# Transposing the attention values there and back in two halves of two query blocks, in place of once for four

## The chip, the cores and the metric

The kernel runs on one core of a Trainium2 chip. The metric is the time of the whole program on the device, in microseconds; lower is better. The engines are named as in the profile: PE (TensorE; PEld is its weight loads), DVE (VectorE), ACT (ScalarE), POOL (GpSimd), SP (SyncE, which issues most DMAs).

## What is computed

Four layers in a row, A, B, A, B, on 2048 tokens of 576 features. A is causal attention in a sliding window of 256 tokens, with 32 heads of 18 features; B is a spectral filter. Both add to their input:

```python
def A(x):                       # x: 2048 x 576
    q, k, v = heads(layernorm(x) @ wqkv)          # 32 heads of 18
    s = q @ k.T * 18 ** -0.5, only where 0 <= query - key < 256
    return x + concat(softmax(s) @ v) @ wo

def B(x):
    X = rfft2(layernorm(x))
    return x + irfft2(X * (w_r + 1j * w_i))
```

The change is in A, so both attention layers meet it.

## The kernel before

**Groups and tiles.** A's 32 heads go in 8 groups of 4 (`n`), its tokens in 16 query tiles of 128 (`i`); x = 16n + i counts 128 such pieces of work. In a layer, projections (`pj`, L1109) make q and k of the groups, later ones while earlier groups are already attended to.

**One piece.** For each of its four heads (`pair`, `hp`) PE makes the scores S of a query tile (L1172, up to 384 keys wide) and DVE their maximum over the keys (L1174: `jk` is a by-product, `m` the result). Ten pieces later, with the maxima folded into q, PE makes the scores again with keys on the partitions (E, L1205), ACT takes exponentials into P (L1206), and POOL clears what the window excludes (L1208, L1211). Scores have three PSUM buffers, E three.

**Values.** `part(x, half)` (L1216) multiplies P with v: U, one PSUM bank of 128 partitions by 512 elements (`bufs=1`), takes four heads of 18 values and a sum in 32 partitions each, by four query tiles of 128. Each call issues matmuls of 128 or 256 queries for the four heads. After the fourth tile DVE transposes U into `us` (L1230, 128x512, in 32x32 blocks), so that the values of a token lie along the free dimension.

**From us to the output.** `later` (L1311) books three steps for bursts 1, 3 and 4 later: `divide` (L1238: DVE takes the reciprocal of the sums, and POOL multiplies, or DVE in the last group), `back` (L1244: DVE transposes us into o, 128x512, L1246), `store` (L1248: DMA of o). The last group's o goes straight into the room of the output projection. At the end of A `out.turn` (L782, three DVE instructions on L787 to L789 for the first blocks) prepares attended values, and `out.early` (L805) starts the output matmuls (`ops`, L802).

**Order.** The order is written by hand; engines run what is issued in that order. `bursts` (L1330) runs bursts of three (tile, pair, hp) steps: one score, three E, two more scores, then either value matmuls or projection steps, then the steps booked for this burst. While projections last, every burst of the set `values` (eight in 22) has the value matmuls of two query tiles and the others projection steps. When the projections are used up (`spread`, from 400.75 us on in layer 1), each burst takes some 8 to 24 value matmuls, and a burst ends ahead of a tile that begins the bank anew (x % 4 == 0). From x = 118 (MIX) on a plain loop without scores follows, `pv` for two tiles behind the exponentials, and then the output matmuls.

**Weights and tables.** `w_load` (L894) reads raw weights of a projection unit into one of two `wraw` buffers; `w_split` (L899) splits them into high and low parts, `wqh` and `wql`, and issues the load for the unit after the next. Late in a layer `const` (L754) puts five tables of the filter into the places of wraw, wqh and wql.

Of the kernel before, what the change touches and what calls it, by code (L numbers as in the profile page):

```python
# [8 lines left out]
F32 = mybir.dt.float32  # L9
F32R = mybir.dt.float32r  # L10
# [7 lines left out]
NF = 290  # L18
NT = 16
# [622 lines left out]
NQ = 8  # L642
# [54 lines left out]
def split_w(nc, raw, h, l, eng_l):  # L697
    nc.scalar.copy(h, raw)
    eng_l.tensor_sub(l, raw, h.bitcast(F32))
# [16 lines left out]
class Out:  # L716
# [36 lines left out]

    def const(self, k):  # L754

        t = ("wraw", "wraw", "wqh", "wqh", "wql")[k]
        d = self.bp.tile([128, 2, NF], F32R, tag=t, name=f"dc{k}", bufs=2)
        self.nc.sync.dma_start(d.bitcast(F32), self.dc_d[:, 2 * k:2 * k + 2].bitcast(F32))
        self.dcs.append(d)

# [105 lines left out]
def layer_a(tc, ident, eps, bp, big, src, dst, wqk_d, wv_d, wo_d, dc_d, gc_d, dram, copy, wvs, second, spectral, share):  # L866

    nc = tc.nc
    V, A, T, P = nc.vector, nc.scalar, nc.tensor, nc.gpsimd
# [14 lines left out]
    if True:  # L884
# [7 lines left out]
        wt, wraws = {}, {}  # L892

        def w_load(i):  # L894
            raw = bp.tile([128, 5, 128], F32, tag="wraw", name=f"wqr{i}", bufs=2)
            nc.sync.dma_start(raw.rearrange("p a b -> p (a b)"), wqk_d[i])
            wraws[i] = raw

        def w_split(i):  # L899
            raw = wraws[i]  # L900
            h = bp.tile([128, 5, 128], F32R, tag="wqh", name=f"wqh{i}", bufs=2)
            l = bp.tile([128, 5, 128], F32R, tag="wql", name=f"wql{i}", bufs=2)
            wt[i] = (h, l)
            split_w(nc, raw, h, l, V if i == 2 else P)
            if i + 2 < 9:
                w_load(i + 2)


        with tc.tile_pool(name="a1", bufs=2) as wp, ExitStack() as banks:
            pps = []  # L910
            if not second:
                wraw = wp.tile([128, 5, D], F32, name="wvraw", bufs=1)
# [163 lines left out]
        with ExitStack() as c2:  # L1076
            wp = c2.enter_context(tc.tile_pool(name="a2", bufs=2))
# [17 lines left out]
            def proj(i, c, bank=0):  # L1095
# [5 lines left out]
                def mm(s, k):  # L1101
                    wk, p, xk = k
                    if s == 7 and c == 2 and 0 < i < 8:
                        w_split(i + 1)
# [109 lines left out]
            us = {}  # L1214

            def part(x, half):  # L1216
                n, i = divmod(x, NT)

                e = i - i % 2
                j = (i - 1, i - 2 + 2 * (i % 2))[half]  # L1220
                q0 = e if j < i else i
                q1 = e + 2 if i - 1 == j else q0 + 1
                for h in range(4):
                    if j >= 0:
                        T.matmul(U[32 * h:32 * h + 19, (q0 % 4) * 128:(q0 % 4) * 128 + 128 * (q1 - q0)], vts[n][:, j, h],  # L1225
                                 pt[n, j][:, h, (q0 - j) * 128:(q1 - j) * 128],
                                 start=j == max(e - 1, 0), stop=j == i or (i == e and j == i - 2), skip_group_check=True)
                if half and i % 4 == 3:
                    us[n, i // 4] = u = wp.tile([128, NT, 32], F32, tag="us", name=f"us{n}_{i}", bufs=1)
                    V.transpose(u, U.rearrange("r (p n) -> r n p", n=NT))  # L1230

            def pv(x):
                part(x, 0)
                part(x, 1)

            os = {}

            def divide(n, c):  # L1238
                u = us[n, c]
                rc = wp.tile([128, NT, 1], F32, tag="rc", name=f"rc{n}_{c}", bufs=2)  # L1240
                V.reciprocal(rc, u[:, :, 18:19])
                (V if n == NQ - 1 else P).tensor_mul(u[:, :, 0:18], u[:, :, 0:18], rc.to_broadcast([128, NT, 18]))

            def back(n, c):  # L1244
                os[n, c] = o = wp.tile([128, NT, 32], F32, tag="o", name=f"o{n}_{c}", bufs=2)
                V.transpose(o, us[n, c])  # L1246

            def store(n, c, engines=None):  # L1248
                o = os[n, c].rearrange("r n p -> r (n p)")
                if n < NQ - 1:  # L1250
                    nc.sync.dma_start(op_d[n, :, c], o)
                    return
                for h in range(4):
                    (engines[h] if engines else nc.sync).dma_start(out.o7[18 * h:18 * h + 18, 512 * c:512 * c + 512], o[32 * h:32 * h + 18])
# [54 lines left out]
            steps = {}  # L1309

            def later(k, n, c):  # L1311
                for lag, f in zip(later.lags, (divide, back, store)):
                    steps.setdefault(k + lag, []).append((f, n, c))
                if c == 3:
                    for h in range(4):
                        steps.setdefault(k + (10 + 2 * h if n < NQ - 2 else 9 + h // 2), []).append((pack, n, h))

            later.lags = 1, 3, 4

            def lasting(p):  # L1320
                x, half = p
# [112 lines left out]
            U = pp.tile([128, 512], F32, tag="U", name="U", bufs=1)  # L1434
# [2 lines left out]
                f()  # L1437
                done += 1
            now = -(-4 * MIX // 3)
            later.lags = 1, 3, 4  # L1440
            ahead = [(max(now, 2 * k - now), f) for k in sorted(steps) for f in steps.pop(k)]
            for k, f in ahead:
                steps.setdefault(k, []).append(f)
# [20 lines left out]

            out.early(0, [bank(k, f"ops0_{k}") for k in ("pj", "S")], slice(0, 4))
            divide(NQ - 1, 3)
            back(NQ - 1, 3)
            store(NQ - 1, 3, (nc.sync, nc.scalar, P, nc.sync))
            out.early(0, None, slice(4, 11))
            out.early(1, [bank("S", f"ops1_{k}") for k in range(2)])  # L1470
# [55 lines left out]
```

## Time and profile before

| what | before |
|---|---|
| time, median of 3 runs | 1332.05 us (1330.12 to 1336.22) |
| time of the profiled execution | 1332.09 us |
| its span in the profile | 1330.0 us |
| first attention, from the first burst to the first output matmul | about 127 to 456.55 us |
| second attention | about 808 to 1137.16 us |
| us transposes (L1230) | 64, median 717 ns |
| o transposes (L1246) | 64, median 707 ns |
| granted TensorE clock, all but start and end | 9 tenths or more |

A row of a timeline gives the start, the duration, the engine, the line, the operation with output and inputs, and in brackets how long the engine stood idle before it and what ended that. Matmuls are pipelined, so the start of the next instruction tells when one is through better than its own duration does. A transpose's duration contains its way out of the engine, which overlaps with the next instruction; its occupancy is the distance to the next start. A row of a group gives busy time, mean duration, and idle time before the group's instructions with what ended most of it.

### The profile page before, as it was taken

What the parts mean: (1) busy time and instruction counts of PE and PEld (TensorE: products, weight loads), DVE (VectorE), ACT (ScalarE), POOL (GpSimd) and SP (SyncE); (2) the same over time, 40 slices, a digit from 0 to 9 for tenths busy, and PEclk for the clock granted to TensorE, in tenths of its full rate; (3) what the DMA queues carried; (4) which work ended last, traced back from release to release, by engine and by line L of the source; (5) the groups of instructions that cost most, each with busy time, mean ns of one, the idle gap of its engine ahead of it and who ended that gap; (6) DMA issues with size and microseconds to landing.
All of it is one profiled execution on the core that took longest, in us unless ns stands there. A gap on an engine that the chain in (4) does not pass through costs nothing.

```text
span 1330.0 us, 33103 instructions
## 1 busy us (share of the span) xinstructions
PE 1295.2 (97%) x10911; PEld 957.5 (72%) x10911; DVE 947.2 (71%) x3132; ACT 753.5 (57%) x1896; POOL 721.8 (54%) x1212
## 2 busy tenths in 40 slices
PE   9999999999999899999999999999999999999998
PEld 8986666566665599975999975666656654897587
DVE  5417888888889677766674148988888887675755
ACT  5622776677767645533355415677766678573233
POOL 2258666676667643566221295567667668213721
PEclk9999999999999999999999999999999999999999
DMA  6856766665657747688873468566656659497884
GB/s 205 215 161 204 220 206 190 214 201 186 188 162 241 222 120 227 191 282 254 265 251 76 102 208 225 184 213 178 192 175 192 189 173 296 140 346 254 283 260 155
DMA packets 179487, 274.22 MB, mean 206 GB/s; under 512 B 67743, under 2 KB 77727, under 8 KB 177989
## 3 DMA queue, kind: packets, MB, share of 16 engines
q1 hardware_dynamic: 166751, 242.45, 58.4%
q0 software_dynamic: 4912, 14.62, 4.3%
q10 hardware_dynamic: 7654, 15.03, 3.2%
q8 instruction: 88, 1.44, 0.5%
q14 instruction: 82, 0.67, 0.2%
HBM read 164.54 MB, written 114.81 MB: 210 GB/s over the span
## 4 chain that ended last, share of the span: by engine, by line
PE 82%; DMA 4%; POOL 4%; DVE 3%; issue 3%; ACT 2%; SPq 1%; DVEq 0%; ACTq 0%; POOLq 0%
PE pj L1109 18%; PE S L1172 13%; PE U L1225 11%; PE vps L1005 9%; PE ops L802 7%; PE E L1205 5%; PE po L274 4%; PE pq L524 3%; PE p L503 2%; PE pi L600 2%; PE pf L274 2%; PE pz L312 1%; POOL ks L1266 1%; POOL qs L1267 1%; DMA yd<-ye 1%
## 5 line engine op out<-in xcount | busy, mean ns | idle before, releaser
L1174 DVE CUSTOM_DVE_ANT_0 jk<-S,mask 128x384 bf16<-128x384 f32 (+2 forms) x1024 | 488.2, 525 | 72.3 <-PE S L1172 35.9
L1206 ACT ACTIVATE P<-E 128x384 f32<-128x384 f32 (+2 forms) x1024 | 408.2, 476 | 171.9 <-PE E L1205 134.4
L1172 PE MATMUL S<-ks,qs 63*128 63x384 f32 (+2 forms) x1024 | 280.1, 374 | 1.3 <-POOL qs L1267 0.3
L1208 POOL TENSOR_SCALAR_AFFINE_SELECT P<-P 128x512 f32<-128x512 f32 x256 | 163.2, 638 | 190.6 <-ACT P L1206 173.8
L1205 PE MATMUL E<-qs,ks 64*128 64x384 f32 (+2 forms) x1024 | 224.7, 372 | 6.4 <-ACT P L1206 3.7
L1172 PEld LDWEIGHTS S<-ks,qs 63*128 63x128 f32 x1024 | 145.6, 184 | 115.2 <-DVE m L1174 87.2
L1225 PE MATMUL U<-P,vq 128*19 128x128 f32 (+1 forms) x3840 | 188.6, 328 | 5.1 <-DVE us L1230 3.3
L1109 PE MATMUL pj<-xh,wqh 128*128 128x512 f32 x360 | 155.4, 432 | 0.4 <-DVE sg L1127 0.2
L1225 PEld LDWEIGHTS U<-P,vq 128*19 128x19 f32 x3840 | 95.6, 98 | 82.6 <-issue 16.0
L1211 POOL TENSOR_SCALAR_AFFINE_SELECT P<-P 128x512 f32<-128x512 f32 x224 | 142.8, 637 | 0.0
L1205 PEld LDWEIGHTS E<-qs,ks 64*128 64x128 f32 x1024 | 115.6, 185 | 22.5 <-ACT P L1206 16.5
L1109 PE MATMUL pj<-xh,wql 128*128 128x512 f32 x360 | 122.1, 416 | 0.0
L1109 PE MATMUL pj<-xl,wqh 128*128 128x512 f32 x288 | 119.6, 415 | 0.0
L802 PE MATMUL ops<-oroom 128*128 128x290 f32 (+1 forms) x812 | 114.0, 297 | 1.7 <-DVE ofree L848 1.2
L802 PEld LDWEIGHTS ops<-oroom 128*128 128x128 f32 x812 | 110.4, 189 | 2.3 <-ACT ofree L836 1.4
L1109 PEld LDWEIGHTS pj<-xh,wqh 128*128 128x128 f32 x360 | 67.7, 188 | 31.2 <-issue 14.0
L1174 DVE DVE_READ_ACCUMULATOR2_ANT m<- 128x1 f32 x1024 | 85.1, 83 | 0.0
L1121 ACT CAST sg<-pj 128x512 fp32r<-128x512 f32 x72 | 42.4, 589 | 72.9 <-PE pj L1109 66.8
L1109 PEld LDWEIGHTS pj<-xh,wql 128*128 128x128 f32 x360 | 64.2, 188 | 21.9 <-issue 10.8
L1230 DVE STREAM_TRANSPOSE us<-U 128x512 f32<-128x512 f32 x64 | 45.8, 716 | 35.8 <-PE U L1225 35.8
L1109 PEld LDWEIGHTS pj<-xl,wqh 128*128 128x128 f32 x288 | 54.2, 188 | 16.8 <-issue 9.1
L789 POOL TENSOR_TENSOR oroom<-oraw,oroom 64x128 fp32r<-64x128 f32 x26 | 13.9, 536 | 95.8 <-issue 46.1
(509 smaller groups left out, 2290.9 us busy)
## 6 DMA issues: line engine op xcount, KB each, us to landing
qk_d<-sg SPq DMA_DIRECT2D x56, 512.0 KB
qs<-qk_d SPq DMA_DIRECT2D x384, 72.0 KB
ks<-qk_d SPq DMA_DIRECT2D x348, 72.0 KB
op_d<-o SPq DMA_DIRECT2D x56, 256.0 KB
v_d<-vt SPq DMA_DIRECT2D x32, 304.0 KB
vq<-v_d SPq DMA_DIRECT2D x16, 608.0 KB
wt<-in_w SPq DMA_DIRECT2D x16, 580.0 KB
ofree<-x SPq DMA_DIRECT2D x16, 580.0 KB
```

The costliest lines, as they stand in the source:

```text
L274: T.matmul(ps[:, c, 0:NF], tail[r] if si == 4 else hl_(si), dcs[b // 2][r, b % 2], start=mi == si == 0, stop=si == 4)
L802: self.nc.tensor.matmul(self.ps[u][n][:, 0:self.n], x, self.w[p][:, (2 * wk + n) * self.n:(2 * wk + n + 1) * self.n], start=first and i == ...
L1005: T.matmul(ps[:, n, 0:288], xT(xk, c), w[:, wk, n * 288:(n + 1) * 288], start=i == 0, stop=i == len(ks) - 1)
L1109: T.matmul(box["ps"].rearrange("r (n p) -> r n p", n=NT) if second else box["ps"], w[:, wk], x, start=s == 0, stop=s == len(ks) - 1)
L1172: T.matmul(ps[:, 0:N], q[b:b + 63, pair, i * 128:i * 128 + 128], k[b:b + 63, pair, lo:hi], start=True, stop=True)
L1174: V.tensor_tensor_reduce(out=jk[:, 0:N], in0=ps[:, 0:N], in1=mask[:, 384 - N:384], scale=1.0, scalar=-3e38, op0=ALU.add, op1=ALU.max, accu ...
L1205: T.matmul(ps[:, 0:nq], k[b:b + 64, pair, j * 128:j * 128 + 128], q[b:b + 64, pair, j * 128:j * 128 + nq], start=True, stop=True)
L1206: A.activation(p[:, hl_, 0:nq], ps[:, 0:nq], AF.Exp, scale=SC)
L1208: P.affine_select(out=p[:, :, 0:128], in_=p[:, :, 0:128], pattern=[[0, 4], [1, 128]], compare_op=ALU.is_ge, fill=0.0, base=0, channel_mult ...
L1211: P.affine_select(out=p[:, :, 256:384], in_=p[:, :, 256:384], pattern=[[0, 4], [-1, 128]], compare_op=ALU.is_gt, fill=0.0, base=0, channel ...
L1225: T.matmul(U[32 * h:32 * h + 19, (q0 % 4) * 128:(q0 % 4) * 128 + 128 * (q1 - q0)], vts[n][:, j, h], pt[n, j][:, h, (q0 - j) * 128:(q1 - j) ...
L1230: V.transpose(u, U.rearrange("r (p n) -> r n p", n=NT))
```

## The change

U is transposed into us in two halves of 128x256, one after each odd query tile: the first half when tiles 0 and 1 of the four are through, the second after tiles 2 and 3. us has two buffers in place of one. o is made by two transposes of 128x256 as well: the first in the third burst after the group's last tile, as before, the second in the fourth, where the store stands too. A half holds pairs of tiles, in runs of 16 tokens of o. To make room, raw weights have one buffer instead of two (the first two of a layer are read into another pool), a load is issued one unit before its use in place of two, and the filter's tables move to other buffers of the same kinds. The matmuls, exponentials, maxima and their order on PE, ACT and POOL are unchanged; DVE gets 64 us and 64 o transposes more.

```diff
@@ -753,8 +753,8 @@
 
     def const(self, k):
 
-        t = ("wraw", "wraw", "wqh", "wqh", "wql")[k]
-        d = self.bp.tile([128, 2, NF], F32R, tag=t, name=f"dc{k}", bufs=2)
+        t = ("wraw", "wqh", "wqh", "wql", "wql")[k]
+        d = self.bp.tile([128, 2, NF], F32R, tag=t, name=f"dc{k}", bufs=2 if k else 1)
         self.nc.sync.dma_start(d.bitcast(F32), self.dc_d[:, 2 * k:2 * k + 2].bitcast(F32))
         self.dcs.append(d)
 
@@ -892,7 +892,7 @@
         wt, wraws = {}, {}
 
         def w_load(i):
-            raw = bp.tile([128, 5, 128], F32, tag="wraw", name=f"wqr{i}", bufs=2)
+            raw = wp.tile([128, 5, 128], F32, name=f"wqr{i}", bufs=1) if i < 2 else bp.tile([128, 5, 128], F32, tag="wraw", name=f"wqr{i}", bufs=1)
             nc.sync.dma_start(raw.rearrange("p a b -> p (a b)"), wqk_d[i])
             wraws[i] = raw
 
@@ -902,8 +902,8 @@
             l = bp.tile([128, 5, 128], F32R, tag="wql", name=f"wql{i}", bufs=2)
             wt[i] = (h, l)
             split_w(nc, raw, h, l, V if i == 2 else P)
-            if i + 2 < 9:
-                w_load(i + 2)
+            if 0 < i < 8:
+                w_load(i + 1)
 
 
         with tc.tile_pool(name="a1", bufs=2) as wp, ExitStack() as banks:
@@ -1225,9 +1225,11 @@
                         T.matmul(U[32 * h:32 * h + 19, (q0 % 4) * 128:(q0 % 4) * 128 + 128 * (q1 - q0)], vts[n][:, j, h],
                                  pt[n, j][:, h, (q0 - j) * 128:(q1 - j) * 128],
                                  start=j == max(e - 1, 0), stop=j == i or (i == e and j == i - 2), skip_group_check=True)
-                if half and i % 4 == 3:
-                    us[n, i // 4] = u = wp.tile([128, NT, 32], F32, tag="us", name=f"us{n}_{i}", bufs=1)
-                    V.transpose(u, U.rearrange("r (p n) -> r n p", n=NT))
+                if half and i % 2:
+                    c, g = divmod(i // 2, 2)
+                    if g == 0:
+                        us[n, c] = wp.tile([128, NT, 32], F32, tag="us", name=f"us{n}_{c}", bufs=2)
+                    V.transpose(us[n, c][:, 8 * g:8 * g + 8], U[:, 256 * g:256 * g + 256].rearrange("r (p a b) -> r a b p", a=8, b=2))
 
             def pv(x):
                 part(x, 0)
@@ -1241,9 +1243,10 @@
                 V.reciprocal(rc, u[:, :, 18:19])
                 (V if n == NQ - 1 else P).tensor_mul(u[:, :, 0:18], u[:, :, 0:18], rc.to_broadcast([128, NT, 18]))
 
-            def back(n, c):
-                os[n, c] = o = wp.tile([128, NT, 32], F32, tag="o", name=f"o{n}_{c}", bufs=2)
-                V.transpose(o, us[n, c])
+            def back(n, c, g):
+                if g == 0:
+                    os[n, c] = wp.tile([128, NT, 32], F32, tag="o", name=f"o{n}_{c}", bufs=2)
+                V.transpose(os[n, c][:, :, 16 * g:16 * g + 16].rearrange("r (a b) p -> r a b p", b=2), us[n, c][:, 8 * g:8 * g + 8])
 
             def store(n, c, engines=None):
                 o = os[n, c].rearrange("r n p -> r (n p)")
@@ -1309,13 +1312,11 @@
             steps = {}
 
             def later(k, n, c):
-                for lag, f in zip(later.lags, (divide, back, store)):
-                    steps.setdefault(k + lag, []).append((f, n, c))
+                for lag, f, *g in ((1, divide), (3, back, 0), (4, back, 1), (4, store)):
+                    steps.setdefault(k + lag, []).append((f, n, c, *g))
                 if c == 3:
                     for h in range(4):
                         steps.setdefault(k + (10 + 2 * h if n < NQ - 2 else 9 + h // 2), []).append((pack, n, h))
-
-            later.lags = 1, 3, 4
 
             def lasting(p):
                 x, half = p
@@ -1437,7 +1438,6 @@
                 f()
                 done += 1
             now = -(-4 * MIX // 3)
-            later.lags = 1, 3, 4
             ahead = [(max(now, 2 * k - now), f) for k in sorted(steps) for f in steps.pop(k)]
             for k, f in ahead:
                 steps.setdefault(k, []).append(f)
@@ -1464,7 +1464,8 @@
 
             out.early(0, [bank(k, f"ops0_{k}") for k in ("pj", "S")], slice(0, 4))
             divide(NQ - 1, 3)
-            back(NQ - 1, 3)
+            for g in range(2):
+                back(NQ - 1, 3, g)
             store(NQ - 1, 3, (nc.sync, nc.scalar, P, nc.sync))
             out.early(0, None, slice(4, 11))
             out.early(1, [bank("S", f"ops1_{k}") for k in range(2)])
```

Three places show how the order moves. The first is PE in layer 1 where the projections are used up, around the end of tile 101 (group 6, tile 5): S are scores named by tile, pair and hp, P6_5 the exponentials whose keys are tile 5 of group 6, and brackets name what an instruction waits for. Before:

```order
L1172 MATMUL S114_1_0_6808<-ks1_1061,qs1_1059 128x384 [waits DVE_49]
L1172 MATMUL S114_1_1_6812<-ks1_1061,qs1_1059 128x384 [waits DVE_49]
L1225 MATMUL U_1590<-P6_5_6623,vq6_5787 19x128 [waits Pool_49]
L1225 MATMUL U_1590<-P6_5_6623,vq6_5787 19x128 x3
L1225 MATMUL U_1590<-P6_5_6623,vq6_5787 19x256 [waits Pool_49]
L1225 MATMUL U_1590<-P6_5_6623,vq6_5787 19x256 x3
L1225 MATMUL U_1590<-P6_4_6586,vq6_5787 19x128 x4
L1172 MATMUL S115_0_1_6836<-ks1_1061,qs1_1059 128x384 [waits DVE_49]
```

And after:

```order
L1172 MATMUL S114_1_0_6857<-ks1_1059,qs1_1057 128x384 [waits DVE_49]
L1172 MATMUL S114_1_1_6861<-ks1_1059,qs1_1057 128x384 [waits DVE_49]
L1225 MATMUL U_1588<-P6_5_6673,vq6_5828 19x128 [waits Pool_49]
L1225 MATMUL U_1588<-P6_5_6673,vq6_5828 19x128 x3
L1225 MATMUL U_1588<-P6_5_6673,vq6_5828 19x256 [waits DVE_49,Pool_49]
L1225 MATMUL U_1588<-P6_5_6673,vq6_5828 19x256 x3
L1225 MATMUL U_1588<-P6_4_6635,vq6_5828 19x128 x4
L1172 MATMUL S115_0_1_6888<-ks1_1059,qs1_1057 128x384
```

The first two U rows are the last matmuls of tile 101, the rest those of tile 102. The instructions are the same; the first U matmul of tile 102 has a wait for DVE in addition, and the score behind it has lost its own.

The second is DVE at the same place: jk and m are the maxima of the score with the same numbers, us6_1 (us6_3 and us6_7 in the names before) the turned U of group 6. Before:

```order
L1174 ISA jk113_1_0_6785,m7_0_6684<-S113_1_0_6783,mask_1050 128x256
L1174 ISA m7_0_6684 128x1
L1246 STREAM_TRANSPOSE o6_0_6791<-us6_3_6679 128x512
L1174 ISA jk114_0_0_6795,m7_0_6684<-S114_0_0_6793,mask_1050 128x384
L1174 ISA m7_0_6684 128x1
L1174 ISA jk114_1_0_6810,m7_0_6684<-S114_1_0_6808,mask_1050 128x384
L1174 ISA m7_0_6684 128x1
L1174 ISA jk114_1_1_6814,m7_0_6684<-S114_1_1_6812,mask_1050 128x384
L1174 ISA m7_0_6684 128x1
L1174 ISA jk115_0_1_6838,m7_0_6684<-S115_0_1_6836,mask_1050 128x384
L1174 ISA m7_0_6684 128x1
```

And after:

```order
L1174 ISA jk113_1_0_6834,m7_0_6733<-S113_1_0_6832,mask_1048 128x256
L1174 ISA m7_0_6733 128x1
L1249 STREAM_TRANSPOSE o6_0_6840<-us6_0_6617 128x16x16
L1174 ISA jk114_0_0_6844,m7_0_6733<-S114_0_0_6842,mask_1048 128x384
L1174 ISA m7_0_6733 128x1
L1174 ISA jk114_1_0_6859,m7_0_6733<-S114_1_0_6857,mask_1048 128x384
L1174 ISA m7_0_6733 128x1
L1174 ISA jk114_1_1_6863,m7_0_6733<-S114_1_1_6861,mask_1048 128x384
L1174 ISA m7_0_6733 128x1
L1232 STREAM_TRANSPOSE us6_1_6869<-U_1588 128x256
L1249 STREAM_TRANSPOSE o6_0_6840<-us6_0_6617 128x16x16
L1174 ISA jk115_0_1_6890,m7_0_6733<-S115_0_1_6888,mask_1048 128x384
```

The whole o of the group before is now a half at its old place and a half one burst later; ahead of that stands the first half of the next us, behind the three maxima of the burst.

The third is DVE at the end of layer 1's attention: L787 to L789 are the three instructions of a `turn`, U here holds the last group's last four tiles, and rc and us7 belong to the last group. Before:

```order
L787 CAST oroom_6830<-oraw0_7212 128x512
L788 TENSOR_TENSOR oroom_6830<-oraw0_7212,oroom_6830 128x384
L789 TENSOR_TENSOR oroom_6830<-oraw0_7212,oroom_6830 64x128
L1246 STREAM_TRANSPOSE o7_2_7676<-us7_11_7638 128x512
L787 CAST oroom_6830<-oraw0_7212 128x512
L788 TENSOR_TENSOR oroom_6830<-oraw0_7212,oroom_6830 128x384
L789 TENSOR_TENSOR oroom_6830<-oraw0_7212,oroom_6830 64x128
L787 CAST oroom_6830<-oraw0_7212 128x512
L788 TENSOR_TENSOR oroom_6830<-oraw0_7212,oroom_6830 128x384
L789 TENSOR_TENSOR oroom_6830<-oraw0_7212,oroom_6830 64x128
L1230 STREAM_TRANSPOSE us7_15_7728<-U_1590 128x512
```

And after:

```order
L788 TENSOR_TENSOR oroom_6882<-oraw0_7268,oroom_6882 128x384
L789 TENSOR_TENSOR oroom_6882<-oraw0_7268,oroom_6882 64x128
L1249 STREAM_TRANSPOSE o7_2_7737<-us7_2_7651 128x16x16
L787 CAST oroom_6882<-oraw0_7268 128x512
L788 TENSOR_TENSOR oroom_6882<-oraw0_7268,oroom_6882 128x384
L789 TENSOR_TENSOR oroom_6882<-oraw0_7268,oroom_6882 64x128
L1249 STREAM_TRANSPOSE o7_2_7737<-us7_2_7651 128x16x16
L1232 STREAM_TRANSPOSE us7_3_7762<-U_1588 128x256
L787 CAST oroom_6882<-oraw0_7268 128x512
L788 TENSOR_TENSOR oroom_6882<-oraw0_7268,oroom_6882 128x384
L789 TENSOR_TENSOR oroom_6882<-oraw0_7268,oroom_6882 64x128
L1232 STREAM_TRANSPOSE us7_3_7762<-U_1588 128x256
```

A half o and the first half of the last us stand between the second and the third turn; before, the one us stood behind all three. On PE the first U matmul of tile 126 waits for that half in the order after.

## The prediction

> **What bounds the kernel now.** I read the page first (shares, chain of waits, costliest groups), then busy times by window, then the timelines of PE and DVE where the change acts.
>
> ```profile
> PE 1295.2 (97%) x10911; PEld 957.5 (72%) x10911; DVE 947.2 (71%) x3132; ACT 753.5 (57%) x1896; POOL 721.8 (54%) x1212
> PE 82%; DMA 4%; POOL 4%; DVE 3%; issue 3%; ACT 2%; SPq 1%; DVEq 0%; ACTq 0%; POOLq 0%
> L1172 PEld LDWEIGHTS S<-ks,qs 63*128 63x128 f32 x1024 | 145.6, 184 | 115.2 <-DVE m L1174 87.2
> L1225 PE MATMUL U<-P,vq 128*19 128x128 f32 (+1 forms) x3840 | 188.6, 328 | 5.1 <-DVE us L1230 3.3
> L1230 DVE STREAM_TRANSPOSE us<-U 128x512 f32<-128x512 f32 x64 | 45.8, 716 | 35.8 <-PE U L1225 35.8
> ```
>
> By the shares PE is the bound. But the score matmuls (S) wait 87.2 us at their weight loads for DVE's maxima (m), which free the three score buffers, and DVE waits 35.8 us for U before its transposes: each waits for the other, and which one is late depends on the stage.
>
> ```profile
> 127.00:400.75 273.75, 270.85 (x2658) 165.86 (x2656) 232.45 (x899) 192.88 (x486) 180.97 (x273) 1.00 0.63 196
> 400.75:435.11 34.36, 33.24 (x366) 18.30 (x365) 32.74 (x127) 27.37 (x70) 27.07 (x41) 1.00 0.77 252
> 1081.22:1115.50 34.28, 33.27 (x366) 18.24 (x365) 32.65 (x127) 27.27 (x70) 26.98 (x41) 1.00 0.79 248
> ```
>
> Columns: window, its length, then busy PE, weight loads, DVE, ACT, POOL. In the main stage (first row, layer 1) DVE is busy 232.45 of 273.75 us and has room. Once the projections are used up (second row, and layer 2 in the third) it is busy 32.74 of 34.36: there DVE is the bound. I call that the late stage. What follows it, up to the first output matmul, is the end of attention.
>
> **The price of a half transpose.** DVE's timeline in the late stage:
>
> ```profile
> 404.14 0.42 DVE L1174 CUSTOM_DVE_ANT_0 jk<-S,mask 128x256 bf16<-128x256 f32 x1
> ...
> 404.49 0.71 DVE L1246 STREAM_TRANSPOSE o<-us 128x512 f32<-128x512 f32 x1
> ...
> 405.12 0.52 DVE L1174 CUSTOM_DVE_ANT_0 jk<-S,mask 128x384 bf16<-128x384 f32 x1
> ...
> 405.57 0.55 DVE L1174 CUSTOM_DVE_ANT_0 jk<-S,mask 128x384 bf16<-128x384 f32 x1
> ...
> 406.05 0.55 DVE L1174 CUSTOM_DVE_ANT_0 jk<-S,mask 128x384 bf16<-128x384 f32 x1
> ...
> 406.53 0.55 DVE L1174 CUSTOM_DVE_ANT_0 jk<-S,mask 128x384 bf16<-128x384 f32 x1
> ```
>
> From start to start a whole transpose takes 0.63 us of DVE (404.49 to 405.12), a 384-wide maximum 0.48 (405.57 to 406.05), a 256-wide one 0.35 (404.14 to 404.49). So 128 elements cost 0.13, and a half transpose 0.63 - 2 x 0.13 = 0.36-0.37; I take 0.36. Bounds: 0.32, exactly half, and 0.63, no cheaper than a whole one. The estimate is next to the 0.35 of the maximum of the same width. [...]
>
> **Late stage, DVE's work.** Eight whole transposes a layer (four us, four o) become sixteen halves: 16 x 0.36 - 8 x 0.63 = +0.7 us, on the engine that is the bound.
>
> **Late stage, a new wait of PE.** U is one PSUM bank. In the order after, the first U matmul of query tiles 102, 106, 110 and 114 waits for DVE; before it waited only for POOL. It writes the other half of the bank than the one being transposed, but the wait holds for the bank. And it stands directly behind the odd tile's matmuls, in the same burst. The price of such a wait is seen where the whole bank begins anew:
>
> ```profile
> 409.51 0.71 DVE L1230 STREAM_TRANSPOSE us<-U 128x512 f32<-128x512 f32 x1
> ...
> 410.37 0.85 PE L1225 MATMUL U<-P,vq 128*19 128x256 f32 x16 [0.28 <-DVE us L1230]
> 411.14 0.28 PE L1185 MATMUL tpm<-ident,m 128*16 128x128 f32 x1
> ```
>
> U started 0.86 us after the transpose did; a half makes that 0.86 - 0.27 = 0.59. Sixteen U matmuls then took 0.77. Next, how long after a score its maximum starts, how long 32 U matmuls run, and what a whole transpose does in the main stage:
>
> ```profile
> 204.36 0.44 PE L1172 MATMUL S<-ks,qs 63*128 63x384 f32 x1
> ...
> 204.84 0.56 DVE L1174 CUSTOM_DVE_ANT_0 jk<-S,mask 128x384 bf16<-128x384 f32 x1 [0.17 <-PE E L1205]
> 205.08 1.50 PE L1225 MATMUL U<-P,vq 128*19 128x256 f32 x32
> ...
> 206.51 0.44 PE L1172 MATMUL S<-ks,qs 63*128 63x384 f32 x1
> ...
> 206.65 0.72 DVE L1230 STREAM_TRANSPOSE us<-U 128x512 f32<-128x512 f32 x1 [0.29 <-PE U L1225]
> ...
> 207.29 0.52 DVE L1174 CUSTOM_DVE_ANT_0 jk<-S,mask 128x384 bf16<-128x384 f32 x1
> ```
>
> A score's maximum starts 0.48 after it (204.36 to 204.84); 32 U matmuls take 1.43 (205.08 to 206.51). The first place, tile 101 to 102, was:
>
> ```profile
> 404.99 1.07 PE L1225 MATMUL U<-P,vq 128*19 128x128 f32 x24
> 405.99 0.44 PE L1172 MATMUL S<-ks,qs 63*128 63x384 f32 x1
> ```
>
> PE ran 24 U matmuls without a stop and gave the next score at 405.99, in time for DVE's maximum at 406.53. Now DVE finishes the burst's three maxima first, then takes the half; PE goes on 0.59 after that start, needs 0.77 for the other 16 matmuls, and DVE can take the next maximum 0.48 after the score: 1.84 us, in which DVE has a half us and a half o to do, 0.72. It idles 1.12. At the second place the same, 1.12; at the third and fourth only eight U matmuls remain (about 0.55, between 0.77 and half of it), and behind the fourth no o stands: 0.59 + 0.55 + 0.48 - 0.72 = 0.90, and 1.26. Together 4.4 us, with 0.7 of work 5.1 a layer, **10.2 in both**. Queued behind the waiting U on PE are the next burst's scores; behind them wait DVE and, through the exponentials, ACT and POOL. Bounds: nothing, if DVE had idled there anyway, to 17, at 0.63 a half: 16 x 0.63 - 8 x 0.63 = 5.0 of work and, by the same steps, 0.85 + 0.85 + 0.63 + 1.26 = 3.6 idle a layer.
>
> **End of attention.** Here DVE's row is: first turned output block, o, second block, third block, us of the last group. The change puts the last group's first half us (tile 125) behind the second block, and U of tile 126 must wait for it.
>
> ```profile
> 454.64 0.71 DVE L1246 STREAM_TRANSPOSE o<-us 128x512 f32<-128x512 f32 x1
> 455.27 0.39 DVE L787 CAST oroom<-oraw 128x512 fp32r<-128x512 f32 x1
> ...
> 456.91 0.43 DVE L787 CAST oroom<-oraw 128x512 fp32r<-128x512 f32 x1
> ```
> ```profile
> 454.76 1.28 PE L1225 MATMUL U<-P,vq 128*19 128x256 f32 x24
> ...
> 456.55 0.40 PE L802 MATMUL ops_pj<-oroom 128*128 128x288 f32 x1
> ```
>
> Half an o from 454.64 ends 455.00, the second block (455.27 to 456.91, 1.64) 456.64, the other half o 457.00; from there 0.59 to U and 1.43 for its 32 matmuls: first output matmul 459.02 in place of 456.55, +2.5. Layer 2:
>
> ```profile
> 1134.80 0.56 DVE L787 CAST oroom<-oraw 128x512 fp32r<-128x512 f32 x1 [2.03 <-DMA oraw<-o_d]
> ...
> 1136.30 0.71 DVE L1246 STREAM_TRANSPOSE o<-us 128x512 f32<-128x512 f32 x1
> 1136.93 0.38 DVE L787 CAST oroom<-oraw 128x512 fp32r<-128x512 f32 x1
> ...
> 1138.26 0.43 DVE L787 CAST oroom<-oraw 128x512 fp32r<-128x512 f32 x1
> ```
> ```profile
> 1135.38 1.28 PE L1225 MATMUL U<-P,vq 128*19 128x256 f32 x24
> ...
> 1137.16 0.40 PE L802 MATMUL ops_pj<-oroom 128*128 128x290 f32 x1
> ```
>
> In the same way 1136.30 + 0.36 + 1.33 + 0.36 + 0.59 + 1.43 = 1140.37, +3.2. But DVE waited 2.03 for a DMA ahead of its first block, and with PE late that load lands earlier beside it; I take off half, 1.0. Sum **4.7**. Bounds: 0, if DVE were ahead of PE, to 5.7. Gains here: PE waits of
>
> ```profile
> 436.55 0.85 PE L1225 MATMUL U<-P,vq 128*19 128x256 f32 x16 [0.82 <-DVE us L1230]
> ...
> 443.33 0.44 PE L1205 MATMUL E<-qs,ks 64*128 64x384 f32 x2 [0.46 <-DVE us L1230]
> ```
>
> become 0.27 shorter each, four in both layers: **-1.1**.
>
> **Main stage.** 25 groups of four tiles a layer. DVE gets 4 x 0.36 - 2 x 0.63 = 0.18 more work a group, 9 us in 50: the upper end, if none of it were hidden. For the gain: at 206.65 the whole transpose puts off the maximum from 206.99 (206.51 + 0.48) to 207.29, 0.30; a half ends at 207.01. If each of the 50 counted that is -15, the lower end. Against it, in 16 groups of 25 the order sets a half o directly behind a half us, behind a wait for U's end, where the whole o stood alone among maxima; in the other nine two halves o are spread over two bursts. Followed by hand burst by burst gains and losses cancel: **0**, with 3 either way, since DVE is not the bound here.
>
> **Raw weights** get one buffer: a load is issued one split later.
>
> ```profile
> L698 ACT CAST wqh<-wqr x2: 726/732/738, 115.9 to 141.4; 128x640 fp32r<-128x640 f32 x2
> dcr<-in_dc POOLq DMA_DIRECT2D x4, 362.5 KB, 5.2
> ```
>
> Splits stand some 25 us apart (115.9, 141.4), the slowest listed landing takes 5.2: nothing. If a load came late PE would stop for up to 5.
>
> **Sum.** Span 1330.0 + 10.2 + 4.7 - 1.1 + 0 = 1343.8; the profiled execution is 1332.09, 2.1 around the span, and 0.04 above the median: **1346**.
>
> **Rivals.** *Faster:* half transposes give DVE back sooner after U, so that scores go on earlier all through the main stage, and the late waits of PE fall where DVE is ahead. At two thirds of the -15, and 2 of the late stage's and the end's 14.9, it gives 1332 - 10 + 2 = 1324; it decides from about 9 us gained in the main stage with the 14.9 nearly gone. For it speaks the 0.30 at 207.29; against it the waits in the order, and DVE's room in the main stage. [...] No run here shows halves yet. 0.07.
> *No change:* the delays are taken up where they land. DVE's maxima run ahead of the late waits, and what is lost in the late stage is won back at the end, where PE waits for POOL, ACT and DMA. With 1 to 6 of the 13.8 left: 1333 to 1338. For it speaks that PE's busy time there is modelled and may hide slack; against it that DVE idles only 1.6 us of 34.36, too little to hide 5. 0.20.
> *Dearer halves:* at 0.50 each the late stage has 2.2 more work and 0.4 less idle time a layer, 3.6 in both, and the end 0.8 more: 1350. Of the 50 x 4 x 0.14 = 28 us more in the main stage a fifth would make it 1356. For it: the halves go through 16-token runs in place of whole rows. 0.10.
>
> **Numbers.** Forecast case 0.63: 1341 to 1350, by the 3 of the main stage and some 2 of the waits. 0.5% is 6.7 us, about what a measurement of this kernel can tell from no change, so 1325.4 and 1338.7 divide the cases. Faster 0.07, same 0.20, slower 0.63 + 0.10 = 0.73. The range 1333 to 1354 leaves out the faster case, the low part of no change and the dear end of the last one.
>
> **What would show it.** In the profile after: half transposes from start to start 0.36; U matmuls with idle time put down to DVE's us, some 0.5 to 1 us at the four late places of each layer; the two late windows 5 us longer with more idle DVE; the first output matmul 2 to 3 us further behind the late stage; the main stage as long as before. A late stage of 34.4 us, or U without such waits, makes the prediction wrong.

## The result, and the profile after

The changed kernel takes 1348.01 us (median of 4 runs, 1347.77 to 1352.3), the kernel before beside it 1331.32 us (4 runs, 1330.12 to 1336.22): 1.0126 times as long, 95% interval 1.0106 to 1.0147. Forecast were 1346 us, within 1333 to 1354, and slower.

First the page of the kernel after: shares, then the groups that answer to those of before.

```profile
PE 1300.3 (97%) x10911; PEld 958.7 (71%) x10911; DVE 959.2 (71%) x3260; ACT 751.7 (56%) x1896; POOL 721.3 (54%) x1212
L1172 PEld LDWEIGHTS S<-ks,qs 63*128 63x128 f32 x1024 | 145.6, 184 | 117.0 <-DVE m L1174 83.4
L1225 PE MATMUL U<-P,vq 128*19 128x128 f32 (+1 forms) x3840 | 193.7, 334 | 13.7 <-DVE us L1232 10.6
L1232 DVE STREAM_TRANSPOSE us<-U 128x256 f32<-128x256 f32 x128 | 57.4, 448 | 48.2 <-PE U L1225 48.2
```

The shares say nothing: PE has 97% as before, DVE 71% as before. One row has moved: U's matmuls stand idle 10.6 us for DVE's us, before 3.3. The page doesn't say at which places; the next view does. The windows are the main stage of layer 1 and the late stages of both layers, cut at the same PE instructions as before. Behind the last bracket stand the granted clock, the DMA share and GB/s.

```profile
128.30:402.15 273.85, 271.80 (x2660) 166.56 (x2659) 235.84 (x950) 192.24 (x486) 182.24 (x274) 1.00 0.63 197
402.15:441.40 39.25, 34.16 (x365) 17.98 (x365) 33.52 (x135) 27.34 (x70) 26.92 (x41) 1.00 0.70 220
1089.10:1128.38 39.28, 34.09 (x366) 17.98 (x365) 33.60 (x135) 27.32 (x70) 27.26 (x41) 1.00 0.71 221
```

The late stage has gone from 34.36 to 39.25 us, while DVE's busy time grew from 32.74 to 33.52 only: the added 4.9 us are 0.8 of work and 4.1 of idle time on the engine that is the bound. The main stage has 3.4 us more DVE work and takes as long as before.

PE issues the same instructions in the same order before and after, so the two traces can be laid side by side instruction by instruction. Borders at the same PE instruction give this table of the profiled executions, in us. "Late" ends with the same last score, "end" inside the first output matmuls, "filter" with the next layer's first score of the main stage.

| kernel | start | main 1 | late 1 | end 1 | filter 1 | main 2 | late 2 | end 2 | rest |
|---|---|---|---|---|---|---|---|---|---|
| before | 126.8 | 274.0 | 34.4 | 31.0 | 341.4 | 273.7 | 34.3 | 31.6 | 176.3 |
| after | 128.3 | 273.8 | 39.3 | 33.9 | 339.9 | 273.8 | 39.3 | 35.8 | 174.9 |
| buffers alone | 127.9 | 273.0 | 34.3 | 32.2 | 340.5 | 273.7 | 34.3 | 31.3 | 174.7 |
| halves at once | 127.4 | 274.7 | 34.5 | 34.8 | 339.2 | 274.1 | 34.6 | 34.1 | 174.5 |
| break | 128.2 | 273.9 | 34.6 | 35.1 | 338.9 | 273.8 | 34.6 | 35.6 | 174.8 |
| wait alone | 127.6 | 277.1 | 38.7 | 34.5 | 340.2 | 276.9 | 38.7 | 36.1 | 176.3 |
| later turns | 127.2 | 273.6 | 39.2 | 32.6 | 339.7 | 273.8 | 39.2 | 31.8 | 175.5 |
| break, turns | 129.4 | 273.2 | 34.6 | 32.9 | 340.0 | 273.7 | 34.6 | 31.9 | 174.5 |
| o halves | 128.4 | 272.6 | 34.3 | 34.2 | 341.5 | 273.1 | 34.4 | 32.7 | 174.6 |
| rows on ACT | 128.3 | 272.7 | 34.4 | 32.1 | 339.4 | 273.6 | 34.2 | 32.5 | 174.5 |
| break, turns, rows | 127.8 | 273.0 | 34.6 | 32.2 | 339.8 | 274.5 | 34.6 | 33.2 | 175.0 |
| o halves, rows | 127.8 | 272.7 | 34.4 | 34.0 | 339.1 | 273.1 | 34.3 | 33.2 | 176.8 |

The late columns agree to 0.3 us between all kernels of a kind. Start, end, filter and rest move by 1 to 3 us between kernels that do the same there. In two of these columns the movement goes with the granted clock, which falls to a half for 3.4 us at some places: in filter 1 of before and o halves (341.4 and 341.5, the other ten 338.9 to 340.5), and in the rest of before, wait alone, later turns and o halves with rows (175.5 to 176.8, the other eight 174.5 to 175.0). The ends have to be read together with the clock too.

Now the first late place, tile 101 to 102, on PE and DVE after:

```profile
406.39 0.41 PE L1225 MATMUL U<-P,vq 128*19 128x128 f32 x8
...
407.65 0.44 DVE L1232 STREAM_TRANSPOSE us<-U 128x256 f32<-128x256 f32 x1
408.02 0.40 DVE L1249 STREAM_TRANSPOSE o<-us 128x256 f32<-128x256 f32 x1
408.24 0.85 PE L1225 MATMUL U<-P,vq 128*19 128x256 f32 x16 [1.44 <-POOL P L1208]
409.02 0.44 PE L1172 MATMUL S<-ks,qs 63*128 63x384 f32 x1
...
409.50 0.56 DVE L1174 CUSTOM_DVE_ANT_0 jk<-S,mask 128x384 bf16<-128x384 f32 x1 [1.07 <-PE E L1205]
```

PE does tile 101's last eight matmuls at 406.39, then stands for 1.44 us until 408.24, which is 0.59 after the half transpose began (407.65). The score follows 0.78 later (409.02), its maximum 0.48 after that (409.50), and DVE has idled 1.07. The bracket names POOL's P, but the releaser is a guess from event times; the other places name us:

```profile
418.07 0.85 PE L1225 MATMUL U<-P,vq 128*19 128x256 f32 x16 [1.10 <-DVE us L1232]
428.05 0.63 PE L1225 MATMUL U<-P,vq 128*19 128x256 f32 x8 [1.10 <-DVE us L1232]
436.20 0.63 PE L1225 MATMUL U<-P,vq 128*19 128x256 f32 x8 [1.21 <-DVE us L1232]
```

And DVE's own rows of the same three places:

```profile
419.32 0.56 DVE L1174 CUSTOM_DVE_ANT_0 jk<-S,mask 128x384 bf16<-128x384 f32 x1 [1.07 <-PE E L1205]
429.08 0.56 DVE L1174 CUSTOM_DVE_ANT_0 jk<-S,mask 128x384 bf16<-128x384 f32 x1 [0.86 <-PE E L1205]
437.23 0.56 DVE L1174 CUSTOM_DVE_ANT_0 jk<-S,mask 128x384 bf16<-128x384 f32 x1 [1.18 <-PE E L1205]
```

The end of attention in layer 2, after; half an o, the second turned block from 1148.74, the other half o, the half us, and tile 126's U, which waits for it:

```profile
1148.37 0.45 DVE L1249 STREAM_TRANSPOSE o<-us 128x256 f32<-128x256 f32 x1
1148.74 0.61 DVE L787 CAST oroom<-oraw 128x512 fp32r<-128x512 f32 x1
...
1150.25 0.45 DVE L1249 STREAM_TRANSPOSE o<-us 128x256 f32<-128x256 f32 x1
1150.62 0.41 DVE L1232 STREAM_TRANSPOSE us<-U 128x256 f32<-128x256 f32 x1
...
1151.17 2.68 PE L1225 MATMUL U<-P,vq 128*19 128x256 f32 x32 [1.74 <-DVE us L1232]
1153.78 0.61 PE L802 MATMUL ops_pj<-oroom 128*128 128x290 f32 x1
```

PE stands 1.74 us, and its 32 matmuls then take 2.61 in place of 1.43: the granted clock is at a half there, as the window shows. Below it the same place in layer 1:

```profile
1152.00:1154.00 2.00, 2.00 (x29) 1.19 (x22) 0.33 (x2) 0.00 (x0) 0.00 (x0) 0.50 0.24 61
```
```profile
462.92 0.41 DVE L1232 STREAM_TRANSPOSE us<-U 128x256 f32<-128x256 f32 x1
...
463.47 2.34 PE L1225 MATMUL U<-P,vq 128*19 128x256 f32 x32 [0.36 <-DVE us L1232]
465.74 0.40 PE L802 MATMUL ops_pj<-oroom 128*128 128x288 f32 x1
```

There PE stands only 0.36 us, since the clock is at a half from 458.42 on and PE is late by itself; but it is again the half us that U waits for last. Counted from the end of the late stage, U of tile 126 starts 2.4 us later than before in layer 1 (22.07 for 19.65) and 2.9 later in layer 2.

### The profile page after: what moved, and what is told of

Its sections match the earlier page's. It is cut to its first block, busy times and chain, and to the rows that moved or that the text cites. A ratio compares the mean times of both kernels' runs of the same rounds, so it can differ in the third digit from the quotient of the medians.

```text
span 1345.7 us, 33245 instructions
## 1 busy us (share of the span) xinstructions
PE 1300.3 (97%) x10911; PEld 958.7 (71%) x10911; DVE 959.2 (71%) x3260; ACT 751.7 (56%) x1896; POOL 721.3 (54%) x1212
## 3 DMA queue, kind: packets, MB, share of 16 engines
q8 instruction: 88, 1.44, 0.5%
## 4 chain that ended last, share of the span: by engine, by line
PE 83%; DMA 5%; DVE 4%; issue 3%; ACT 2%; POOL 2%; SPq 1%; DVEq 0%; ACTq 0%; POOLq 0%
PE pj L1109 19%; PE S L1172 13%; PE U L1225 11%; PE vps L1005 9%; PE ops L802 7%; PE E L1205 5%; PE po L274 4%; PE pq L524 2%; PE p L503 2%; PE pf L274 2%; PE pi L600 2%; PE pz L312 1%; DMA ofree<-o 1%; DVE jk L1174 1%; ACT P L1206 1%
## 5 line engine op out<-in xcount | busy, mean ns | idle before, releaser
L1225 PE MATMUL U<-P,vq 128*19 128x128 f32 (+1 forms) x3840 | 193.7, 334 | 13.7 <-DVE us L1232 10.6
L1232 DVE STREAM_TRANSPOSE us<-U 128x256 f32<-128x256 f32 x128 | 57.4, 448 | 48.2 <-PE U L1225 48.2
L1109 PEld LDWEIGHTS pj<-xh,wqh 128*128 128x128 f32 x360 | 67.6, 188 | 33.2 <-issue 14.2
L1109 PEld LDWEIGHTS pj<-xh,wql 128*128 128x128 f32 x360 | 64.2, 188 | 21.5 <-issue 10.6
L789 POOL TENSOR_TENSOR oroom<-oraw,oroom 64x128 fp32r<-64x128 f32 x26 | 13.9, 535 | 100.7 <-ACT oroom L787 50.8
```

The costliest lines, as they stand in the source:

```text
L1109: T.matmul(box["ps"].rearrange("r (n p) -> r n p", n=NT) if second else box["ps"], w[:, wk], x, start=s == 0, stop=s == len(ks) - 1)
L1232: V.transpose(us[n, c][:, 8 * g:8 * g + 8], U[:, 256 * g:256 * g + 256].rearrange("r (p a b) -> r a b p", a=8, b=2))
```

## The experiments

The theory: a half transpose reads a bank whose other half U goes on to write, so U waits for DVE; where U follows in the same burst and DVE is the bound, both lose. The rivals: the 128 more DVE instructions cost the time, or the moved buffers and loads do.

**Buffers alone**: the kernel before with the change's edits to raw weights and tables.

```diff
-        t = ("wraw", "wraw", "wqh", "wqh", "wql")[k]
+        t = ("wraw", "wqh", "wqh", "wql", "wql")[k]
...
-            raw = bp.tile([128, 5, 128], F32, tag="wraw", name=f"wqr{i}", bufs=2)
+            raw = wp.tile([128, 5, 128], F32, name=f"wqr{i}", bufs=1) if i < 2 else bp.tile([128, 5, 128], F32, tag="wraw", name=f"wqr{i}", bufs=1)
...
-            if i + 2 < 9:
-                w_load(i + 2)
+            if 0 < i < 8:
+                w_load(i + 1)
```

> The kernel before with only the change's other half: one raw-weight buffer, loads one split later, the filter's tables in other buffers; all transposes whole. My theory (PE's wait for the half-transposed bank) gives these moves nothing: 1330 to 1334 us, and the start of the program as long as before. If they cost something, the 1.1 us by which the first 100 us of the changed kernel were longer show here too. The rival that the moves of memory and loads make the change slow would give 1340 to 1348.

Measured: 1330.88 us (median of 10; before 1331.07, ratio 1.0000, 0.9984 to 1.0017). The moves cost nothing that can be told; that rival is out.

**Halves at once**: the change, with both half transposes of U after the fourth tile.

```diff
-                if half and i % 2:
-                    c, g = divmod(i // 2, 2)
...
+                if half and i % 4 == 3:
+                    c = i // 4
+                    us[n, c] = wp.tile([128, NT, 32], F32, tag="us", name=f"us{n}_{c}", bufs=2)
+                    for g in range(2):
+                        V.transpose(us[n, c][:, 8 * g:8 * g + 8], U[:, 256 * g:256 * g + 256].rearrange("r (p a b) -> r a b p", a=8, b=2))
```

> The changed kernel, with both half transposes of U issued together after the fourth tile: as many instructions on DVE as in the change, but no U matmul waits for a half while it writes the other. By my theory the two late stages lose only DVE's work of 0.7 us and four times 0.1 us of longer waits at whole banks, about 1 us a layer in place of 4.9 and 5.0, and the end of attention is within 1 us of before: 1333 to 1337. The rival that the 128 instructions more on DVE are the cost leaves it at 1346 to 1349.

Measured: 1335.82 us (median of 6, ratio 1.0053, 1.0026 to 1.0080). Its late stage, as a window:

```profile
402.10:436.64 34.54, 33.33 (x364) 18.30 (x364) 32.84 (x134) 27.23 (x70) 26.86 (x41) 1.00 0.74 235
```

34.54 us with 14 half transposes in this stage, where the change has 15 (the whole programs have equally many): the change's 4.9 us are not the instructions. The late stages lose 0.2 and 0.4 us where about 1 was expected; why it is less is not shown, for two halves in a row take 0.70 us of DVE (1111.35 to 1112.05), nearly twice 0.36. The end of attention was missed: 34.8 and 34.1 us with no wait of tile 126 in it. PE waits 2.5 and 1.1 us there for the last rows of maxima, and the granted clock is at a half for 6.8 us in each layer (446.74 to 453.57, 1136.23 to 1143.06); I had counted on neither. That the total lies in the expected range is partly luck: the ends are 6.3 us longer than before, and filter 1 and the rest, with no half clock, 4.0 shorter.

**Break**: the change, with a burst ending ahead of every even tile.

```diff
-                    while parts and (took < 430 or source(parts[0]) < e[0][0] - 3 if spread else took == 0 or parts[0][0] % 2 or parts[0][1]):
+                    while parts and (took < 500 or source(parts[0]) < e[0][0] - 3 if spread else took == 0 or parts[0][0] % 2 or parts[0][1]):
...
-                        if took and half == 0 and (x % 4 == 0 or x % NT == 1):
+                        if took and half == 0 and (x % 2 == 0 or x % NT == 1):
```

> The changed kernel, but in the late stage a burst ends ahead of every even tile (and takes up to 24 matmuls more than 430 allowed, 500 in the table's units), so that the scores of the next burst stand between the half transpose and the U matmuls that wait for it. By my theory the late stages go from 39.2 us to 35 to 36 and the end of attention stays 2 to 4 us a layer longer than before: 1338 to 1342. If DVE's work or the loads were the cause it stays at 1346 to 1349.

Measured: 1338.10 us (median of 4, ratio 1.0067, 1.0042 to 1.0093). The waits for DVE are all still in the program, but a burst's scores stand ahead of them now:

```profile
402.07:436.66 34.59, 34.22 (x364) 18.95 (x364) 32.94 (x135) 27.05 (x70) 26.54 (x41) 1.00 0.78 240
```

Late stage 34.59, a little below the expected 35 to 36; the ends, 35.1 and 35.6, are 4 us longer than before, the upper edge of what was expected. What costs in the late stage is not that U waits but that nothing stands between the transpose and the wait. The break by itself, on the kernel before, was not tried.

**Wait alone**: the kernel before with whole transposes, and one copy of one element a partition out of U after the second tile.

```diff
+                if half and i % 4 == 1:
+                    V.tensor_copy(wp.tile([128, 1], F32, tag="uw", name=f"uw{n}_{i}", bufs=2), U[:, 0:1])
                 if half and i % 4 == 3:
```

> The kernel before, whole transposes, plus one copy of one element a partition out of U after the second tile of each four: it adds nearly no work to DVE (32 copies a layer) but gives the U matmuls of the even tiles the same 14 waits for DVE as the change. Worked from the rows of before: idle time of DVE in the late stage 1.48 + 0.85 + 0.63 + 1.26 = 4.2 us and some 0.6 of copies a layer, and 2.5 and 2 to 3 us at the two ends: 1342 to 1348. The rival that the number and length of the transposes is the cost gives 1331 to 1335.

Measured: 1354.73 us (median of 4, ratio 1.0179, 1.0155 to 1.0204), longer than the change itself. Its first late place:

```profile
410.44 0.15 DVE L1229 COPY uw<-U 128x1 f32<-128x1 f32 x1
410.74 0.84 PE L1225 MATMUL U<-P,vq 128*19 128x256 f32 x16 [1.42 <-POOL P L1208]
411.52 0.44 PE L1172 MATMUL S<-ks,qs 63*128 63x384 f32 x1
...
411.99 0.56 DVE L1174 CUSTOM_DVE_ANT_0 jk<-S,mask 128x384 bf16<-128x384 f32 x1 [1.40 <-PE E L1205]
```

A copy of 0.15 us costs DVE 1.40 idle (1.48 expected). The late stages take 38.7 us, 4.4 more than before against an expected 4.8. The miss is in the main stage, 3.1 us a layer where I expected nothing: there a DVE instruction that waits for U's end after the first two tiles does hold up something. In the change the same wait stands in the main stage, which still takes 274. So the shorter second half must give about as much back; that balance is inferred from the two kernels and not taken apart. The ends grow by 3.5 and 4.5, more than expected too; the granted clock is at a half in them for 3.4 and 6.8 us.

**Later turns**: the change, with the turned blocks one tile later, so that one of them and not two stands ahead of the last group's first half.

```diff
-                if t - OB - 5 in (0, 1, 2):
-                    out.turn(t - OB - 5, V)
+                if t - OB - 6 in (0, 1, 2):
+                    out.turn(t - OB - 6, V)
```

> The changed kernel with the three turned output blocks issued one query tile later, so that only the first of them, and not the first two, stands on DVE ahead of the half transpose that U of tile 126 waits for. By my theory that wait sets the end of attention: U of tile 126 starts 1.3 to 1.6 us sooner in each layer, the ends shrink by 1.3 to 2.4 each: 1343 to 1346 us. The rival that the ends are long from the granted clock (0.5 for some 6 us there) and from the wait for the last rows of maxima alone leaves 1347 to 1349. The late stages stay at 39.2 to 39.6 us.

Measured: 1341.73 us (median of 4, ratio 1.0070, 1.0046 to 1.0094), some 6 us faster than the change. Tile 126 in layer 2:

```profile
1145.59 1.50 PE L1225 MATMUL U<-P,vq 128*19 128x256 f32 x32 [0.77 <-DVE us L1232]
1147.02 0.40 PE L802 MATMUL ops_pj<-oroom 128*128 128x290 f32 x1
```

The wait is 0.77 in place of 1.74, the 32 matmuls take 1.43 again, and the ends go from 33.9 and 35.8 to 32.6 and 31.8, near those of before (31.0, 31.6). The total is below the expected 1343 to 1346, because not all of the gain of 1.4 and 3.9 is the order's: the half clock in the ends, 6.8 us in each layer of the change, is down to 3.4 in layer 1 and gone in layer 2. What the order does is seen on DVE from the last transpose that waits for U ahead of the turned blocks to the start of tile 126's U: 457.16 to 463.47 and 1145.25 to 1151.17 in the change, 456.90 to 461.48 and 1140.64 to 1145.59 here, 1.7 and 1.0 us less (1.3 to 1.6 expected). The other half of the gain, some 2.6 us (an estimate, 1.4 and 3.9 less 1.7 and 1.0), goes with the clock, so the rival that makes the clock lengthen the ends is right for that part.

**Break and later turns** together are the two edits above.

> The burst break ahead of every even tile and the later turns together, on the changed kernel. If the two waits are separate and both real, the gains add: 1338.1 with the break alone, less 2 to 4 for the ends: 1334 to 1336 us. If only the late stage's wait was real, 1337 to 1339. Below 1331 only if halves are good for something that the waits have hidden so far.

Measured: 1334.11 us (median of 10, ratio 1.0019, 1.0001 to 1.0037). The two gains add up within the intervals: of the change's 1.26% the break takes 0.59 and the later turns 0.56, which would leave 0.11%, and 0.19% is left.

**o halves**: the kernel before with o alone in two halves.

```diff
-                for lag, f in zip(later.lags, (divide, back, store)):
-                    steps.setdefault(k + lag, []).append((f, n, c))
+                for lag, f, *g in ((1, divide), (3, back, 0), (4, back, 1), (4, store)):
+                    steps.setdefault(k + lag, []).append((f, n, c, *g))
...
+                V.transpose(os[n, c][:, 8 * g:8 * g + 8], us[n, c][:, 8 * g:8 * g + 8])
```

> The kernel before with only o in two half transposes, in the third and the fourth burst; us whole, no new wait for PE. DVE's work in the late stage grows by 4 x 0.36 x 2 - 4 x 0.63 = 0.4 us a layer; in the main stage smaller pieces may hide better. My theory gives 1330 to 1333 us, with U waits as before. The rival that half transposes themselves, by their number, are what costs: half of the change's 16, about 1339.

Measured: 1333.36 us (median of 10, ratio 1.0010, 0.9994 to 1.0026): no difference that can be told, and far from the rival's 1339.

**Rows on ACT's queue**: the kernel before, with the last row of maxima sent from ACT.

```diff
-                    (nc.sync if n or c > 1 else nc.scalar).dma_start(q[63::64, pair, c * 512:c * 512 + 512].bitcast(F32), mt[8 * pair:8 * pair + 8].bitcast(F32))
+                    (nc.scalar if (n, c) == (NQ - 1, 3) else nc.sync if n or c > 1 else nc.scalar).dma_start(q[63::64, pair, c * 512:c * 512 + 512].bitcast(F32), mt[8 * pair:8 * pair + 8].bitcast(F32))
```

> The kernel before, but the last group's last row of maxima (mt, 4 KB each) goes out on ACT's queue in place of SP's, where it stands behind 256 to 512 KB of other transfers. In the kernel before PE's loads of E wait 0.71 and 1.09 us for it near the end of the two attentions, in the changed one 1.77 and 1.59. If the order within SP's queue is what delays it, both waits go below 0.3 us and the time is 1329 to 1331; if the transfer engines are simply full (their share is 0.9 to 1.0 there), waits and time stay as before, 1331.

Measured: 1334.66 us (median of 10, ratio 1.0019, 1.0000 to 1.0038). The expected 1329 to 1331 was missed. PE's list of waits has none for these rows any more (before two, 2.0 us together), so the order of SP's queue did delay them; but the ends are not shorter (32.1, 32.5). The edit puts another wait in the place of the old one:

```profile
439.05 1.08 ACTq L1189 DMA_DIRECT2D qs<-mt  x2
...
440.16 0.67 ACT L751 CAST oroom<-ofree 128x576 fp32r<-128x576 f32 x1 [1.15 <-issue]
...
441.28 0.44 PE L1205 MATMUL E<-qs,ks 64*128 64x384 f32 x1 [1.40 <-ACT P L1206]
```

While ACT issues the two transfers it does no other work for 1.15 us, its exponentials come later by that, and PE stands 1.40 us for P, in layer 2 as well (1120.65). So this run doesn't show what the wait for the rows was worth in the kernel before.

**Two last combinations**, tried for a version faster than both: break, turns and rows on ACT; and o halves with rows on ACT.

> The changed kernel with the burst break, the later turns and the last rows of maxima on ACT's queue. With both waits gone it stood at 1334; if the wait of 2 to 3 us of PE for those rows, which the break made longer, is the rest of the difference from before, this gives 1330 to 1332. If that wait lay beside other work, as in the kernel before, it stays at 1333 to 1336. Faster than the kernel before by more than 3 us only if halves have a use of their own.

> The kernel before with o alone in halves and the last rows of maxima on ACT's queue: no new wait for PE. In the run with o halves alone the main stages were 1.4 and 0.6 us shorter than in the kernel before, and the ends longer by 3.2 and 1.1 with a wait of 2.0 us for the rows. If the two add up, 1328 to 1330, the fastest so far; if they are within what one execution differs from another, 1331 to 1334.

Measured: 1333.47 us (12 runs, ratio 1.0033, 1.0019 to 1.0048) and 1333.23 us (12 runs, 1.0017, 1.0002 to 1.0032), with before at 1330.16. Both fall in the range that was to mean no gain. Three of their four ends have the new wait of 1.4 us for ACT's P, so they don't show what halves would be worth without any wait; they show that nothing tried is faster than the kernel before.

## Why the prediction was right

- **Price of a half.** 0.36 us forecast; 0.37 measured (407.65 to 408.02).
- **Late stage.** 5.1 us a layer forecast; 4.9 and 5.0 measured. The steps hold one by one: 0.59 from the transpose to U, forecast 0.59; idle time of DVE at the four places 1.07, 1.07, 0.86, 1.18, forecast 1.12, 1.12, 0.90, 1.26. Two small things were off. The sum goes from eight whole transposes to sixteen halves, but the stage has seven and fifteen, so by its own price the work is 1.0 and not 0.7; measured are 0.8 and 0.95. And PE itself stands 1.1 to 1.4 us at these places, not the 0.5 to 1 named as a sign. Wait alone shows that the wait suffices, halves at once that the work doesn't, break that the place in the order decides.
- **End of attention.** 4.7 less 1.1, so 3.6, forecast; 2.9 + 4.2 = 7.1 measured. The mechanism was right as far as it goes: U of tile 126 waits for the half us behind the second turned block, and starts 2.4 and 2.9 us later than before, where the sum has it start 2.8 (457.59 for 454.76) and, with 1.0 taken off for the DMA, 2.6 later. Two terms were mis-sized. The first is the half clock, which was not in the sum: it stretched tile 126's U from 1.43 to 2.3 and 2.6 us and lies over other matmuls of both ends as well. The second is the gains of -1.1, which didn't come. The waits at whole banks of 0.82 and 0.79 are 0.75 after. And the 0.46 at 443.33, read as a wait for a transpose, was none: the matmul there is E, which reads qs and not us, and in the changed kernel the same instruction waits 1.52 for the last row of maxima (450.64, `DMA qs<-mt`).
- **Main stage.** 0 forecast, -0.2 and +0.2 measured. The reason given, that DVE has room, was too simple: wait alone loses 3.1 there. That losses and gains just cancel is not taken apart by any run, so the 0 is partly luck.
- **Raw weights and tables.** Nothing forecast, nothing measured (buffers alone).
- **What the sum lacked.** The start is 1.6 us longer and the two filter stages are 1.5 and 1.3 shorter in the profiled execution. The filter stages go with the clock: the kernel before has a stretch of 3.4 us at half in each (from 629.59 and from 1226.93), the changed one has none there. The start is 1.6 and 1.5 longer in o halves and rows on ACT too, which load weights as the kernel before does, so it is not the change's.

So the total, 1346 for 1348, is closer than its parts: the ends came out 3.5 us dearer than forecast, the filter stages 2.8 cheaper than before, and that these nearly cancel is luck.

The rivals: faster and no change failed on the late stages, which absorbed nothing; dearer halves on 0.37.

## What to carry to other kernels

Before one instruction is cut in two, look at what its operands are guarded by: here the program's wait for U holds for its whole PSUM bank, so reading half of it early gives the writer of the other half a wait that the whole never had (at the four late places of layer 1 PE stands 1.44, 1.10, 1.10 and 1.21 us). Count each new wait at its place in the order: with a burst's scores ahead of it (break) it costs the late stage 0.2 to 0.3 us, directly behind its own releaser on two engines that work in turn (late stage) it costs the whole round trip, 1.1 us for 0.37 us of work. And an instruction is as early as what stands ahead of it in its engine's queue: with two turned blocks ahead of a half transpose, the matmuls that wait for it start 2.4 and 2.9 us later.

## What the runs showed of the hardware

In eleven of the twelve profiled executions the granted clock falls to a half, for 3.4 or 6.8 us at a time, at one to four places ahead of the program's end; rows on ACT has none. The 9 tenths in the table of before is a mean over slices of 33 us, in which such a stretch is lost. In windows of 2 us, two of the kernel before, at the filter stages, and then two of the kernel after, at the ends of attention (the granted clock is the number after the last bracket):

```profile
630.00:632.00 2.00, 2.00 (x11) 1.98 (x10) 0.00 (x0) 0.94 (x2) 0.34 (x2) 0.50 0.96 310
1228.00:1230.00 2.00, 2.00 (x9) 1.18 (x8) 1.34 (x2) 0.00 (x0) 0.50 (x1) 0.50 0.90 294
```
```profile
460.00:462.00 2.00, 1.64 (x12) 0.89 (x16) 1.94 (x5) 1.11 (x4) 0.65 (x1) 0.50 0.95 206
1138.00:1140.00 2.00, 2.00 (x20) 0.91 (x20) 1.60 (x3) 0.87 (x2) 1.99 (x5) 0.50 0.72 204
```

Ahead of the first of each pair stand these waits of PE, the longest in the 12 us ahead of it. The clock falls at 629.59, 1.4 us after the first wait ends, and at 458.42, 7.8 us after the second:

```profile
628.18 1.66 PE L274 MATMUL wo<-dc,half 128*128 128x290 f32 x10 [2.01 <-DVE half L268]
```
```profile
450.64 0.44 PE L1205 MATMUL E<-qs,ks 64*128 64x384 f32 x2 [1.52 <-DMA qs<-mt]
```

What brings the half clock on stays open; no run tried it by itself. A lull right ahead is neither always there nor enough: in the 3.41 us ahead of the two falls, as long as the stretch from 629.59 to 633.00 lasts, PE was busy for 1.41 and 2.95 us, and in the changed kernel it was busy for 1.47 us from 1240.10 to 1243.51 without a fall behind it (granted clock 1.00 from there to 1247.00).

What the clock is worth shows in the 63 executions of the kernel before that ran beside the experiments: the 21 with a mean granted clock of 0.998 or more have a median of 1329.6 us, the 15 with 0.995 or less 1332.5. The four of the changed kernel have 0.991 to 0.995, so some 2 to 3 of its 16.7 us (an estimate from these medians) go with the clock; one profile of each kernel doesn't show whether the change itself brings that on.
